# q features of batches 5 to 7 made token-major and transposed by the DMA crossbar, q of batches 0 and 1 loaded by whole rows, and a new order of all steps

## The chip, the cores and the metric

The kernel runs on one core of a Trainium2 chip. The engines of a core work side by side and meet at semaphores: PE (TensorE, matmuls; PEld is its loading of weights), DVE (VectorE), ACT (ScalarE), POOL (GpSimd) and SP (SyncE, which issues DMAs). DMAs issued from POOL and from SP run on the core's 16 DMA engines. The metric is the device time of one execution in microseconds (us), as a median of several runs. A profile is one further execution; its span is the time from its first to its last instruction.

## What is computed

The reference is a linear attention with an exponential feature map, followed by a feed-forward network with a squared ReLU.

```python
# q, k, v: 8 batches x 8 heads x 576 tokens x 64;  w_phi: 64 x 128
def phi(x):
    proj = np.einsum('bhsd,df->bhsf', x, w_phi)
    proj = proj - np.max(np.abs(proj), axis=-1, keepdims=True)
    return np.concatenate([np.exp(proj), np.exp(-proj)], axis=-1)
q_p, k_p = (phi(q), phi(k))
kv = np.einsum('bhsf,bhsd->bhfd', k_p, v)
z = np.sum(k_p, axis=2)
num = np.einsum('bhsf,bhfd->bhsd', q_p, kv)
den = np.einsum('bhsf,bhf->bhs', q_p, z)[..., None] + 1e-06
# then, with the heads side by side as x: 4608 tokens x 512
h = np.maximum(x @ w_in, 0.0)          # w_in: 512 x 2048
out = (h * h @ w_out).astype(np.float32)   # w_out: 2048 x 512
```

## The kernel before, in words

**Tiles.** A batch has 576 tokens and eight heads. Two heads lie side by side in 128 columns, so a batch of q or k is 18 blocks of 128 tokens by 128 columns: 16 for the first 512 tokens and two for the last 64 tokens of all heads. Loads are issued from POOL and turn float32 into bf16 on the way (`load`, L253 for the 512 tokens and L261 for the 64). The code speaks of five groups `c` (of q) or `g` (of k) in a batch: four of four blocks, and the last, number 4, of two blocks with the 64 tokens.

**Attention, `attention(b)`.** For each batch:
- q and k are turned so that the 64 features of a head lie on partitions. Batches 0 and 1 do this on PE (`pe_transposes`, L328, with a copy out by DVE or ACT); from batch 2 on it is one DMA transpose through the crossbar for each of q and k, issued from SP (`transposed`, L338).
- For k, `project` (L354; L381 in batch 0) multiplies by w_phi with tokens on the output's partitions ("token-major"); DVE takes the largest absolute value of each token and head (L409), ACT makes the two exponentials kp and kn (L415, L397 in batch 0). v is scaled by the exponential of the maximum (L442, on DVE; batches 0 and 1 may do it on POOL), and `kv_ops` (L472, L477) gives kv and z.
- For q, `qmax_ops` makes the same token-major projection (L354, L507 in batch 0) only for DVE's maximum (L514) and a small exponential of it, `en`; the bank is free after that. `q_ops` then makes the projection a second time, with the 128 features on partitions ("feature-major", L549, two matmuls of 512 columns for a group), and ACT makes qp and qn of it (L564, twice).
- `out_ops` multiplies qp with kv (NA, L579), DVE scales by `en` (L591), qn with kv is added (NB, L579), DVE takes the reciprocal of the denominator (L599) and divides (L603), and the result xo is transposed into xT by a DMA on SP (L637; in batch 0 on PE, L619 and L628). The last 64 tokens of all batches go to xS.

**Feed-forward.** Chunk c holds batch c's first 512 tokens; chunk 8 holds the 64 last tokens of all batches. F1 (L719; L730 for chunk 0 in pieces) multiplies by w_in; ACT or DVE takes the ReLU (L694, L696), DVE or, in chunks 0 and 1, POOL squares it (L703); F2 (L784; L748 for the last tile in halves) multiplies by w_out, and ACT or DVE copies the result out (L195, L197) for a store from SP (L803, L800, L771). The FFN of chunk c stands between the attention of later batches.

**The order.** The code above only lists steps with what they read and write (`add`). The order in which they are issued is a written-out list, `ORDER`; each engine takes its steps in that order and waits at each until its inputs are there. `BASES` gives each PSUM bank group its bank, `STATES` picks one of two engines for the steps that have a choice, `GATES` makes a load of batch 2 and later wait for a named step, and `FILL` puts idle matmuls (L853) on a tile of zeros ahead of some PE steps. The numbers in `add`'s cost field serve the search that wrote the list; they do not run.

**q's loads in batches 0 and 1 (`load_q`, L284).** They come in halves: token pairs 0 and 1 of each row of four first (128 of 256 columns), then pairs 2 and 3. From batch 2 on q is loaded in four pieces of whole rows (L273).

## Time and profile before

| | |
|---|---|
| median of 3 runs | 355.15 us (354.94 to 355.79) |
| profiled execution: span, first to last instruction | 353.0 us |
| instructions in the span | 8396 |
| PE busy | 340.7 us, 97% of the span |
| DVE busy | 276.1 us, 78% |
| ACT busy | 226.8 us, 64% |
| POOL busy | 96.6 us, 27% |
| DMA packets | 96101, 39.59 MB, mean 112 GB/s |
| granted TensorE clock | 1.000 |

For the profiled execution itself the profile gives the span of 353.0 us; it stands 2.15 us under the median of the runs.

How to read it: the page gives the busy time of each engine, then the span in 40 slices with one digit for each engine (9 means busy for 90% or more), then the DMA queues, then the chain of work that ended last, followed back from the last instruction, and then the costliest groups of instructions. In a group, `out<-in` are the program's tile names, then partitions x elements and type, the count, and after the first bar the busy time in us and the mean of one instruction in ns; after the second bar stands the idle time of the engine ahead of them, and what ended it. A timeline line has the start in us, the duration in us, engine, line, operation, tiles and count. An SP or POOL line with a DMA is its issue; the landing is later.

### The profile page before, as it was taken

Reading aid. Unit: us, or ns where it says so; the run is one execution under the profiler, and the core shown is the slowest. Engines: PE = TensorE matmul, PEld = TensorE weight load, DVE = VectorE, ACT = ScalarE, POOL = GpSimd, SP = SyncE. Lnnn points to the kernel's source line nnn. Section 1 sums busy time; section 2 is a strip of 40 time slices with the busy share of each in tenths; the row PEclk is TensorE's granted clock in tenths of the full one; section 3 lists DMA queues with packets and bytes.
Section 4 is the critical chain, followed back from the end, with each engine's and each line's share of the span. In section 5 each row is a group of like instructions: output and inputs, shape, how many; then the busy total and the mean of one; then the engine's idle time right before and its main releaser. Section 6 shows DMA issues by size and latency. Waiting matters only on the chain.

```text
span 353.0 us, 8396 instructions
## 1 busy us (share of the span) xinstructions
PE 340.7 (97%) x3367; PEld 192.2 (54%) x3400; DVE 276.1 (78%) x524; ACT 226.8 (64%) x428; POOL 96.6 (27%) x144
## 2 busy tenths in 40 slices
PE   8889999999999999999999999999999999999995
PEld 5679875544654554545445654455555544444452
DVE  4999998899979988989678888799988727736210
ACT  4999887499688875785678577869676211340301
POOL 8745350488429300297001820000000000000000
PEclk9999999999999999999999999999999999999999
DMA  9999999899989976899354995600211211010105
GB/s 102 177 200 202 196 107 155 134 142 175 182 169 150 155 141 155 160 111 158 79 129 84 120 187 111 146 20 21 53 40 53 47 51 48 30 59 2 59 3 176
DMA packets 96101, 39.59 MB, mean 112 GB/s; under 512 B 64576, under 2 KB 91584, under 8 KB 96064
## 3 DMA queue, kind: packets, MB, share of 16 engines
q0 software_dynamic: 45216, 18.36, 45.6%
q1 hardware_dynamic: 50528, 20.42, 26.5%
q8 instruction: 26, 0.43, 0.5%
q10 hardware_dynamic: 320, 0.30, 0.3%
q14 instruction: 11, 0.09, 0.1%
HBM read 36.77 MB, written 9.44 MB: 131 GB/s over the span
## 4 chain that ended last, share of the span: by engine, by line
PE 79%; DVE 8%; ACT 6%; DMA 3%; issue 2%; SPq 0%; POOL 0%; DVEq 0%; ACTq 0%; POOLq 0%
PE psum L784 30%; PE psum L719 28%; PE psum L579 5%; PE psum L354 4%; PE psum L472 3%; PE psum L730 3%; PE psum L549 2%; DVE va L442 2%; DMA xq<-in_q_dram 1%; DVE mq L514 1%; ACT kp L415 1%; ACT kn L415 1%; DMA out_dram<-ot 1%; DVE mk L388 1%; DVE h L703 1%
## 5 line engine op out<-in xcount | busy, mean ns | idle before, releaser
L784 PE MATMUL psum<-wout,h 128*128 128x512 bf16 x527 | 128.4, 379 | 3.2 <-issue 1.3
L719 PE MATMUL psum<-xT,win 128*128 128x512 bf16 x448 | 106.1, 379 | 0.1
L694 ACT ACTIVATE hr<-psum 128x512 bf16<-128x512 f32 x96 | 55.3, 596 | 46.3 <-PE psum L719 24.3
L784 PEld LDWEIGHTS <-h 128*128 128x128 bf16 x560 | 50.2, 98 | 55.2 <-issue 2.0
L719 PEld LDWEIGHTS <-win 128*128 128x128 bf16 x512 | 47.4, 97 | 53.7 <-issue 3.1
L703 DVE TENSOR_TENSOR h<-hr 128x512 bf16<-128x512 bf16 x143 | 55.9, 415 | 16.4 <-ACT hr L694 15.6
L564 ACT ACTIVATE qp<-psum 128x1024 bf16<-128x1024 f32 (+1 forms) x40 | 37.4, 940 | 21.9 <-PE psum L549 21.5
L514 DVE TENSOR_REDUCE mq<-psum 128x8 f32<-128x1024 f32 (+1 forms) x40 | 44.1, 1110 | 4.0 <-PE psum L354 3.2
L409 DVE TENSOR_REDUCE mk<-psum 128x8 f32<-128x1024 f32 (+1 forms) x35 | 38.1, 1110 | 3.1 <-PE psum L354 3.1
L415 ACT ACTIVATE kp<-psum 128x1024 bf16<-128x1024 f32 (+1 forms) x35 | 32.8, 937 | 11.6 <-DVE mk L409 8.9
L564 ACT ACTIVATE qn<-psum 128x1024 bf16<-128x1024 f32 (+1 forms) x40 | 37.4, 939 | 1.3 <-PE psum L579 1.0
L696 DVE TENSOR_SCALAR hr<-psum 128x512 bf16<-128x512 f32 x48 | 32.6, 686 | 6.5 <-PE psum L719 5.2
L253 POOL DMA_DIRECT2D xv<-in_v_dram x26 | 19.4, 763 | 51.3 <-DVE va L442 48.0
L415 ACT ACTIVATE kn<-psum 128x1024 bf16<-128x1024 f32 (+1 forms) x35 | 32.8, 936 | 0.0
L442 DVE TENSOR_TENSOR va<-xv,va 64x256 bf16<-64x256 bf16 (+2 forms) x68 | 30.4, 462 | 1.6 <-ACT va L434 0.8
L591 DVE TENSOR_TENSOR psum<-psum,en 128x520 f32<-128x520 f32 (+1 forms) x40 | 27.6, 699 | 3.9 <-PE psum L579 2.5
L603 DVE TENSOR_TENSOR xo<-psum,rden 128x512 bf16<-128x512 f32 (+1 forms) x40 | 27.3, 686 | 1.0 <-DVE rden L599 0.2
L197 ACT ACTIVATE ot<-psum 128x512 f32<-128x512 f32 x18 | 10.7, 595 | 27.1 <-PE psum L784 27.1
L195 DVE COPY ot<-psum 128x512 f32<-128x512 f32 x17 | 11.5, 684 | 15.2 <-PE psum L784 7.9
L253 POOL DMA_DIRECT2D xk<-in_k_dram x28 | 20.6, 743 | 8.4 <-ACT va L428 4.0
L472 PE MATMUL psum<-va,kp 128*128 128x65 bf16 x256 | 19.6, 193 | 0.8 <-DVE va L442 0.4
L472 PE MATMUL psum<-va,kn 128*128 128x65 bf16 x256 | 19.6, 193 | 0.0
(69 smaller groups left out, 403.4 us busy)
## 6 DMA issues: line engine op xcount, KB each, us to landing
out_dram<-ot SPq DMA_DIRECT2D x32, 256.0 KB, 2.7
xk<-in_k_dram POOLq DMA_DIRECT2D x26, 128.0 KB, 4.3
xq<-in_q_dram POOLq DMA_DIRECT2D x24, 128.0 KB, 5.5
xv<-in_v_dram POOLq DMA_DIRECT2D x24, 128.0 KB, 4.2
win<-in_moe_w_in_dram POOLq DMA_DIRECT2D x4, 512.0 KB, 11.3
wout<-in_moe_w_out_dram POOLq DMA_DIRECT2D x4, 512.0 KB, 11.7
xq<-in_q_dram POOLq DMA_DIRECT2D x4, 256.0 KB, 5.8
xv<-in_v_dram POOLq DMA_DIRECT2D x2, 512.0 KB, 9.3
```

Of the source, the lines that this page charges most:

```text
L253: pin(nc.gpsimd.dma_start(out=x[:, a * 512 : z * 512].rearrange("p (h x) -> p h x", x=4 * D), in_=src[b][2 * a : 2 * z, 0:512, :].rearrang ...
L409: pin(nc.vector.tensor_reduce(out=mk_view(g), in_=ps2(pj)[:, :, : n * Fd].rearrange("p e (i f) -> p e i f", f=Fd), axis=AX.X, op=ALU.max, ...
L415: pin(nc.scalar.activation(out=dst[slot][:, :, :n, :].rearrange("p e i f -> p e (i f)"), in_=ps2(pj)[:, :, : n * Fd], func=ACT.Exp, scale= ...
L442: pin(engine().tensor_tensor(out=t[:, :, :D].rearrange("p m (x c) -> p m x c", c=2), in0=x.rearrange("p (m x c) -> p m x c", m=n, c=2), in ...
L472: pin(nc.tensor.matmul(out=o[:, sg, hi, :], lhsT=(kp, kn)[sg][kgroup[pr]][:, j % 2, 2 * hi + j // 2, :], rhs=va[s2][sg][:, 8 * pr + 4 * hi ...
L514: pin(nc.vector.tensor_reduce(out=mqb[:, c, :, :n], in_=ps2(pj)[:, :, : n * Fd].rearrange("p e (i f) -> p e i f", f=Fd), axis=AX.X, op=ALU ...
L564: pin(nc.scalar.activation(out=o, in_=i_, func=ACT.Exp, scale=sgn))
L694: pin(nc.scalar.activation(out=hr[sl], in_=ps1(g), func=ACT.Relu))
L696: pin(nc.vector.tensor_scalar(out=hr[sl], in0=ps1(g), scalar1=0.0, scalar2=None, op0=ALU.max))
L703: pin(engine().tensor_tensor(out=dst, in0=i_, in1=i_, op=ALU.mult))
L719: pin(nc.tensor.matmul(out=o, lhsT=win[mc // 4][:, kc, mc % 4 * P : (mc % 4 + 1) * P], rhs=x, start=(kc == 0), stop=(kc == KC - 1)))
L784: pin(nc.tensor.matmul(out=ps1(g), lhsT=h2[c % 2][mc // 4][:, mc % 4, tt * P : (tt + 1) * P], rhs=wout[mc // 4][:, mc % 4, :], start=(mc = ...
```

## The change

- In batches 5 to 7 (`LATE`), a q group's second, feature-major projection is gone. Instead, `qmax_ops` keeps the bank of the token-major projection after the maximum, and ACT makes both exponentials of it into a tile `qe` (two of them, in turn). One DMA transpose from SP (step Xf) turns its 16 blocks of 128x128 into the feature-major `qf`, of which qp and qn are now the two halves; for the last group of a batch it is two transposes of four blocks. In these batches `qmax_ops` stands beside `out_ops` group by group.
- q of batches 0 and 1 is loaded like k, in whole rows; batch 0's in two pieces of two head pairs. PE's transposes of q take the blocks in the order that this gives.
- The ring of k feature tiles has 6 slots for 7. The tile of the last output half lies over the first `qe`; an unused tile is dropped.
- `ORDER`, `BASES`, `STATES`, `GATES` and `FILL` are new throughout. By the new `STATES` and order, POOL has 17 squares (1 before) and 8 scalings of v (0 before), the ReLUs are 92 on ACT and 52 on DVE (96 and 48 before), kv's copies 23 and 9 (19 and 13), the output copies 20 and 15 (18 and 17). `FILL` has 28 idle matmuls (76 before). POOL's first load is k's head pairs 2 and 3 of batch 0 (256 KB in bf16); before it was head pair 0 (128 KB).

```diff
--- before.py
+++ after.py
@@ -165,7 +165,7 @@
     warm = sb("warm", [256])
     xk, xq, xv = ring("xk", 2, [36 * D]), ring("xq", 2, [36 * D]), ring("xv", 2, [36 * D])
     kT, qT = ring("kT", 2, [18, P]), ring("qT", 2, [18, P])
-    NKP = 7
+    NKP = 6
     kp, kn = ring("kp", NKP, [2, 4, P]), ring("kn", NKP, [2, 4, P])
     va = [[sb(f"va{b}{s}", [40, D1 + 1]) for s in range(2)] for b in range(2)]
     mk, mq = ring("mk", 2, [36], F32), ring("mq", 2, [5, 2, 4], F32)
@@ -175,16 +175,17 @@
     NXT = 2
     LENT = 2
     assert B * S == NCH * TCH and NCH == B + 1 and S == TCH + 64
-    qp, qn = ring("qp", NQP, [8 * P]), ring("qn", NQP, [8 * P])
+    LATE, NQE = 5, 2
+    qf, qe = ring("qf", NQP, [2, 8 * P]), ring("qe", NQE, [2, 8 * P])
+    qp, qn = [t[:, 0, :] for t in qf], [t[:, 1, :] for t in qf]
     xo = ring("xo", 5, [8 * D])
     rden = ring("rden", 5, [8], F32)
     xT = [ring(f"xT{c}", 2, [4, 2, P]) for c in range(NXT)]
     xS = sb("xS", [4, KC, P])
-    mkn = sb("mkn", [36], F32)
     hr = ring("hr", 4, [TCH])
     h2 = [ring(f"h2{c}_", 4, [4, TCH]) for c in range(2)]
     ot = ring("ot", 3, [DM], F32)
-    otl = sb("otl", [DM], F32)
+    otl = qe[0][:, 0, :].bitcast(F32)
 
     plan = Plan()
     add = plan.add
@@ -264,36 +265,12 @@
                 add("POOL", (0.72, 0), fn, w=[(tag, b % 2, "s", hi)], dma=(LD["s"], SW_IN, "ld", late(b)),
                     release=release, what=tag + "s")
 
-    def load_q(b, jjs=(0, 1), single=True, release=False, prs=((0, 4),)):
-
-        x = xq[b % 2]
-        if b >= 2:
-            for a, z in prs:
-                def fn(a=a, z=z):
-                    pin(nc.gpsimd.dma_start(
-                        out=x[:, a * 512 : z * 512].rearrange("p (h x) -> p h x", x=4 * D),
-                        in_=q[b][2 * a : 2 * z, 0:512, :].rearrange("h (p j) d -> p h (j d)", j=4)))
-                old = sorted({pr // 2 for pr in range(a, z)}) if b < 4 else []
-                add("POOL", (0.72, 0), fn, w=[("xq", b % 2, "g", pr) for pr in range(a, z)] + [("xq", b % 2, jj) for jj in old]
-                    + [("xq", b % 2, jj, y) for jj in old for y in range(3)],
-                    dma=(work(b, LD["main"] * (z - a) / 4), SW_IN, "ld", late(b)), release=release, what="xq")
-            jjs = ()
-        for jj in jjs:
-            for a, z in prs:
-                def fn(jj=jj, a=a, z=z):
-                    pin(nc.gpsimd.dma_start(
-                        out=x[:, jj * 1024 + a * 256 : jj * 1024 + z * 256].rearrange("p (h x) -> p h x", x=128),
-                        in_=q[b][2 * a : 2 * z, 0:512, :].rearrange("h (p j) d -> p h (j d)", j=4)[:, :, jj * 128 : jj * 128 + 128]))
-                add("POOL", (0.72, 0), fn, w=([("xq", b % 2, jj)] if z == 4 else []) + [("xq", b % 2, jj, y) for y in range(a, min(z, 3))],
-                     dma=(work(b, LD["main"] / 8 * (z - a)), SW_IN, "ld", late(b)), release=release, what="xq")
-        if single:
-            load(q, xq, b, "xq", prs=(), release=release)
+    def load_q(b, single=True, release=False, prs=((0, 4),)):
+
+        load(q, xq, b, "xq", prs=prs, single=single, release=release)
 
     def of(tag, b, us):
-        if tag == "xq" and b >= 2:
-            return [(tag, b % 2, "g", pr) for pr in range(4)] + [(tag, b % 2, "s", hi) for hi in range(2)]
-        qs = [("xq", b % 2, u, a) for u in us if u != "s" for a in range(3)] if tag == "xq" else []
-        return qs + [(tag, b % 2, u) for u in us if u != "s"] + [(tag, b % 2, "s", hi) for u in us if u == "s" for hi in range(2)]
+        return [(tag, b % 2, u) for u in us if u != "s"] + [(tag, b % 2, "s", hi) for u in us if u == "s" for hi in range(2)]
 
     def load_win(i):
         def fn():
@@ -308,7 +285,7 @@
         add("POOL", (0.72, 0), fn, w=[("wout", i)], dma=(LD["w"], SW_IN, "ld", "first"), what="wout")
 
 
-    kslot, qslot, xslot = [0], [0], [0]
+    kslot, qslot, xslot = [0], [0, 0], [0]
 
     def t_of(g):
         return [16, 17] if g == 4 else [4 * g + i for i in range(4)]
@@ -325,6 +302,8 @@
             def fn():
                 tp = ps1(g).bitcast(BF16)
                 for i, t in enumerate(blocks):
+                    if tag == "xq" and t < 16:
+                        t = t % 8 * 2 + t // 8
                     pin(nc.tensor.transpose(out=tp[:, i * P : (i + 1) * P], in_=x[:, t * P : (t + 1) * P], identity=ident))
             add("PE", pe_cost(n, 0.056), fn, r=of(tag, b, srcs) + ["ident"], opens=g, w=[g], what="T" + tag)
             def fn():
@@ -336,7 +315,7 @@
         def transposed(x, xt, tag, ttag):
             def fn():
                 pin(nc.sync.dma_start_transpose(out=xt, in_=x))
-            add("SP", (2.8 if tag == "xk" else 3.4, 0), fn, r=of(tag, b, (0, 1, "s") if tag == "xq" else (0, 1, 2, 3, "s")),
+            add("SP", (2.8 if tag == "xk" else 3.4, 0), fn, r=of(tag, b, (0, 1, 2, 3, "s")),
                 w=[(ttag, s2, t) for t in range(18)], dma=(3.6, HW_IN, "x", "kq"), what="X" + tag)
 
         if not pe_in:
@@ -496,6 +475,8 @@
                 return [8 * (c // 2) + h for h in range(8)]
             return [(8 * (c // 2) + 4 * (c % 2) + i) if pe_in else 8 * (c % 2) + 2 * i + c // 2 for i in range(4)]
 
+        qfeat = {}
+
         def qmax_ops(c):
             ts = q_ts(c)
             n = min(len(ts), 4)
@@ -514,7 +495,32 @@
                 pin(nc.vector.tensor_reduce(
                     out=mqb[:, c, :, :n], in_=ps2(pj)[:, :, : n * Fd].rearrange("p e (i f) -> p e i f", f=Fd),
                     axis=AX.X, op=ALU.max, apply_absolute_value=True))
-            add("DVE", dve_cost(2 * n * Fd), fn, r=[pj], w=[("mq", s2, c)], closes=pj, what="Mq")
+            turned = b >= LATE
+            add("DVE", dve_cost(2 * n * Fd), fn, r=[pj], w=[("mq", s2, c)] + [pj] * turned, closes=None if turned else pj, what="Mq")
+            if turned:
+                slot, se = qslot[0] % NQP, qslot[1] % NQE
+                qslot[0] += 1
+                qslot[1] += 1
+                qfeat[c] = slot
+                for u, sgn in enumerate((1.0, -1.0)):
+                    def fn(u=u, sgn=sgn):
+                        i_, o = ps2(pj)[:, :, : n * Fd], qe[se][:, u, : 2 * n * Fd]
+                        if c == 4:
+                            o, i_ = o.rearrange("p (i e f) -> p e i f", e=2, f=Fd), i_.rearrange("p e (i f) -> p e i f", f=Fd)
+                        else:
+                            o = o.rearrange("p (e x) -> p e x", e=2)
+                        pin(nc.scalar.activation(out=o, in_=i_, func=ACT.Exp, scale=sgn))
+                    add("ACT", act_cost(2 * n * Fd), fn, r=[pj], w=[pj, ("qe", se, u)], closes=pj if u else None, what="Eq")
+                def fn():
+                    if c == 4:
+                        for u in range(2):
+                            pin(nc.sync.dma_start_transpose(out=qf[slot][:, u, : 4 * P].rearrange("f (x p) -> f x p", p=P),
+                                                            in_=qe[se][:, u, : 4 * Fd]))
+                    else:
+                        pin(nc.sync.dma_start_transpose(out=qf[slot].rearrange("f u (x p) -> f (u x) p", p=P),
+                                                        in_=qe[se].rearrange("p u x -> p (u x)")))
+                add("SP", (2.5 if c < 4 else 2.0, 0), fn, r=[("qe", se, u) for u in range(2)], w=[("qp", slot), ("qn", slot)],
+                    dma=(3.2 * n / 4, HW_IN, "x", "kq"), what="Xf")
 
             if c < 4:
                 def fn():
@@ -528,8 +534,6 @@
                             out=enb[0:64, 4, :].rearrange("p (i e h) -> p e i h", e=2, h=2)[:, :, :, hi],
                             in_=mqb[64 * hi : 64 * hi + 64, 4, :, :2], func=ACT.Exp, scale=-2.0))
                     add("ACT", act_cost(4), fn, r=[("mq", s2, 4)], w=[("en", s2, 4, hi)], what="en")
-
-        qfeat = {}
 
         def q_ops(c):
             ts = q_ts(c)
@@ -647,7 +651,7 @@
             for jj in range(2):
                 for hh in range(2):
                     ts = [8 * jj + 4 * hh + i for i in range(4)]
-                    pe_transposes(xq[s2], "xq", "qT", ts, [jj], qTb[:, ts[0] : ts[-1] + 1, :])
+                    pe_transposes(xq[s2], "xq", "qT", ts, [2 * hh, 2 * hh + 1], qTb[:, ts[0] : ts[-1] + 1, :])
             pe_transposes(xq[s2], "xq", "qT", [16, 17], ["s"], qTb[:, 16:18, :])
             qmax_ops(0)
             q_ops(0)
@@ -663,7 +667,7 @@
                 for jj in range(2):
                     for hh in range(2):
                         ts = [8 * jj + 4 * hh + i for i in range(4)]
-                        pe_transposes(xq[s2], "xq", "qT", ts, [jj], qTb[:, ts[0] : ts[-1] + 1, :])
+                        pe_transposes(xq[s2], "xq", "qT", ts, [2 * hh, 2 * hh + 1], qTb[:, ts[0] : ts[-1] + 1, :])
                 pe_transposes(xq[s2], "xq", "qT", [16, 17], ["s"], qTb[:, 16:18, :])
             for g in (4, 0, 1, 2, 3):
                 kgroup_ops(g)
@@ -677,10 +681,14 @@
             v_ops(2, 4)
             kv_ops(2)
             kv_ops(3)
+            if b < LATE:
+                for c in range(5):
+                    qmax_ops(c)
             for c in range(5):
-                qmax_ops(c)
-            for c in range(5):
-                q_ops(c)
+                if b < LATE:
+                    q_ops(c)
+                else:
+                    qmax_ops(c)
                 out_ops(c)
 
 
@@ -812,9 +820,8 @@
 
     add("POOL", (0.45, 0.6), f_ident, r=["ident0"], w=["ident"], what="ident")
     load(k, xk, 0, "xk", prs=((1, 2), (2, 4)), single=False)
-    load_q(0, jjs=(0,), single=False)
+    load_q(0, prs=((0, 2), (2, 4)))
     load(v, xv, 0, "xv", prs=((0, 4),))
-    load_q(0, jjs=(1,))
     for i in range(4):
         load_win(i)
     load(k, xk, 1, "xk")
@@ -858,120 +865,116 @@
 
 
 ORDER = [
-    4, 3, 0, 1, 5, 9, 13, 15, 2, 6, 12, 8, 14, 40, 10, 41, 11, 7, 42, 64, 44, 43, 19, 65, 46, 18, 66, 45, 109, 16,
...
+    4, 3, 14, 12, 1, 5, 74, 9, 0, 11, 85, 13, 6, 2, 86, 75, 76, 78, 8, 87, 39, 89, 79, 77, 88, 90, 10, 63, 40, 15,
...
 ]
 BASES = (
...
 )
 STATES = (
...
 )
 GATES = {
...
 }
 FILL = {
-    40: (0, 15, 0), 42: (0, 3, 0), 64: (0, 4, 0), 66: (0, 6, 0), 109: (0, 3, 0), 144: (0, 6, 0), 53: (0, 5, 0),
-    77: (3, 2, 0), 155: (7, 19, 0), 158: (7, 5, 0), 127: (2, 2, 0), 149: (6, 1, 0), 161: (6, 5, 0),
+    74: (3, 15, 0), 76: (3, 1, 0), 41: (3, 4, 0), 52: (2, 3, 0), 140: (5, 4, 0), 132: (4, 1, 0),
 }
```

15 lines of the change are left out of this document (7 added, 8 removed), and 188 rows, old and new, of tables (GATES, ORDER).

## The prediction

> **What bounds the kernel now.** I read the page first: busy time, slices, chain.
>
> ```profile
> span 353.0 us, 8396 instructions
> PE 340.7 (97%) x3367; PEld 192.2 (54%) x3400; DVE 276.1 (78%) x524; ACT 226.8 (64%) x428; POOL 96.6 (27%) x144
> ...
> DVE  4999998899979988989678888799988727736210
> ACT  4999887499688875785678577869676211340301
> ...
> PEclk9999999999999999999999999999999999999999
> ...
> PE 79%; DVE 8%; ACT 6%; DMA 3%; issue 2%; SPq 0%; POOL 0%; DVEq 0%; ACTq 0%; POOLq 0%
> ```
>
> PE is busy for 97% of the span and carries 79% of the chain; its clock is granted in full throughout. DVE and ACT stand at 9 in the first slices only. So I cut the span into windows (columns: PE, weight loads, DVE, ACT, POOL busy us; clock; DMA share; GB/s).
>
> ```profile
> 0.00:25.00 25.00, 21.29 (x287) 15.91 (x288) 20.19 (x45) 19.90 (x48) 17.15 (x28) 1.00 1.29 157
> 25.00:50.00 25.00, 24.41 (x427) 21.15 (x427) 24.21 (x52) 23.18 (x44) 12.01 (x17) 1.00 1.25 173
> 50.00:75.00 25.00, 24.68 (x310) 14.64 (x311) 22.50 (x41) 16.91 (x32) 9.57 (x16) 1.00 1.10 144
> 75.00:100.00 25.00, 24.71 (x255) 13.40 (x256) 22.67 (x42) 21.50 (x39) 14.49 (x21) 1.00 1.25 170
> 100.00:150.00 50.00, 49.08 (x514) 26.35 (x518) 45.72 (x78) 37.97 (x73) 17.52 (x26) 1.00 1.01 155
> 150.00:200.00 50.00, 49.00 (x478) 25.94 (x478) 40.73 (x79) 35.50 (x67) 21.11 (x32) 1.00 0.80 114
> 200.00:250.00 50.00, 49.20 (x466) 25.62 (x470) 43.73 (x78) 37.88 (x70) 4.78 (x8) 1.00 0.53 97
> ```
>
> Three stages. Up to 50 us DVE and ACT are both nearly full: they feed PE, and PE's busy time contains fillers and short waits. From 50 to 100 us DVE is 90% full, ACT less. From 100 us on PE idles 2.7 us in 150 (0.92, 1.00 and 0.80).
>
> Prices come from the groups of the page (the last number before the second bar is the mean in ns; the last two are in the full list of groups) and from the chain, where back-to-back matmuls show their real spacing.
>
> ```profile
> L694 ACT ACTIVATE hr<-psum 128x512 bf16<-128x512 f32 x96 | 55.3, 596 | 46.3 <-PE psum L719 24.3
> L703 DVE TENSOR_TENSOR h<-hr 128x512 bf16<-128x512 bf16 x143 | 55.9, 415 | 16.4 <-ACT hr L694 15.6
> L564 ACT ACTIVATE qp<-psum 128x1024 bf16<-128x1024 f32 (+1 forms) x40 | 37.4, 940 | 21.9 <-PE psum L549 21.5
> L514 DVE TENSOR_REDUCE mq<-psum 128x8 f32<-128x1024 f32 (+1 forms) x40 | 44.1, 1110 | 4.0 <-PE psum L354 3.2
> L853 PE MATMUL psum<-warm 128*128 128x248 bf16 x76 | 11.7, 298 | 1.1 <-DVE warm L234 1.1
> L703 POOL TENSOR_TENSOR h<-hr 128x512 bf16<-128x512 bf16 x1 | 1.0, 1041 | 1.5 <-DVE hr L696 1.5
> ```
>
> ```profile
> 71.06 2.59 PE psum L719 x12
> ...
> 269.38 0.54 PE psum L549 x4
> ```
>
> A 512-column matmul costs PE 0.216 us (2.59/12). The feature product (L549, two matmuls for a token group) costs 0.27 (0.54 for two groups).
>
> **The change, part by part.** The sum is made against the profiled execution: its span is 353.0 us, and the median of the runs, 355.15, is 2.15 above it; I add that back at the end.
>
> *Feature products removed.* In batches 5 to 7, 15 groups lose their L549 products: 12 whole ones x 0.27 and 3 half ones x 0.14 = 3.7 us. They stand where PE idles 1 us in 50, so they come off the end: -3.7.
>
> *Exponentials.* Thirty activations on the token-major projection replace thirty on the feature-major one, same size (0.94 each): ACT 0. They hold the projection's bank pair longer, through the maximum (1.11) and both exponentials, while the second pair that the feature product took is gone. Cost 0; the cover is that fewer pairs are open in all.
>
> *Fifteen crossbar steps, 18 instructions, on SP's queue.* The nearest rows are q's own transposes (18 blocks of 128x128; the new ones have 16) and the output's (4 blocks; the last group's two have 4 each):
>
> ```profile
> L338 SPq DMA_TRANSPOSE qT<-xq x6: 2671/2784/7034, 50.2 to 217.4; - x6
> ...
> DMA to landing us min/median/max: 4.6/5.3/9.7
> ```
>
> ```profile
> L637 SPq DMA_TRANSPOSE xT<-xo x28: 1188/1217/2485, 60.5 to 283.9; - x28
> ...
> DMA to landing us min/median/max: 2.3/2.7/6.5
> ```
>
> So a whole group takes some 2.5 us of SP (2.67 x 16/18) and lands 4.3 (quiet: 4.6 less a ninth of 2.67) to 9.7 us after its issue; a last group 2 x 1.2 of SP and lands after 3.5. SP gets 12 x 2.5 + 6 x 1.2 = 37 us of work more; queued behind are stores and the xo transposes, whose consumers come later. What counts is how much PE work the new order puts between a step and the numerator product that reads it. Adding PE's prices along that order: batch 5 has 10 to 15 us, batch 6 has 6.6, 9.5, 5.4, 6.6 and, in its last group, 2.0; batch 7 has 14.2, 3.4, 4.4, 6.1 and 5.9. Two fall short: batch 6's last group by 3.5 - 2.0 and batch 7's second by 4.3 - 3.4, together 2.4, of which the matmul group that is under way at the issue (0.86, half of it on average) covers part. At the median landing of 5.3 three do (4.3 us in all). Bounds 0 to 4.3; I take +1.5, since DMA is at 0.5 and less by then.
>
> *The ramp, which the new order changes most.* I add the mean durations along each engine's order up to two places that the trace times by DVE's reciprocals, batch 0's last token group and batch 2's first:
>
> ```profile
> 41.35 0.19 DVE L599 RECIPROCAL rden<-psum 64x8 f32<-64x8 f32 x1
> ...
> 92.66 0.20 DVE L599 RECIPROCAL rden<-psum 128x8 f32<-128x8 f32 x1
> ```
>
> To the first place before has 37.9 us of ACT work, 37.9 of DVE and 22.6 of PE (fillers left out): 41.35 is ACT's work plus 3.4 of start, and PE has lost 18.7. After has 42.4 of ACT, 38.5 of DVE and 25.0 of PE: ACT's work plus 3.4 gives 45.8. The first load is now k's 256 KB for two head pairs where it was 128 KB for one:
>
> ```profile
> 1.25 1.55 POOL L253 DMA_DIRECT2D xk<-in_k_dram  x2 [0.80 <-POOLq L989]
> 4.44 0.24 PEld L328 LDWEIGHTS <-xk 128*128 128x128 bf16 x4 [0.57 <-DMA xk<-in_k_dram]
> ```
>
> The first 128 KB took 3.2 us to use; the second half of a 256 KB load is bounded by its share of the issue, 1.55/2 = 0.8, above and 0 below; I take 0.8. So 46.6, and PE has lost 21.6: +2.9. Between the two places before has 50.5 of DVE work in 51.3 us against 48.6 of PE: DVE sets the pace, and PE loses 2.7. After has 36.9 of DVE (16 squares and 8 scalings of v go to POOL) and 37.4 of ACT against 40.8 of PE: PE sets the pace, nothing is lost. I take -2.0 of the 2.7, since some short waits will stay. Ramp: +0.9; bounds -2 (ACT's start hidden) to +4 (DVE's relief worth nothing, some more waits).
>
> *POOL.* Sixteen squares x 1.04 and eight scalings (six as long as a square, two of twice its length): 25 us, nearly all before 100 us. POOL is busy for 53 us of that time, so it stays under 80; queued behind each are loads, of which those of win and wout stand ten and more groups ahead of their first matmul. Cost 0 where these arrive on time; bounds below under the rivals.
>
> *Fillers.* 48 of 76 go, 48 x 0.105 (248 columns at 0.216/512) = 5.0 us of PE. All lie before 28 us, where PE waits for ACT and DVE: 0 on the path. If PE was bound there they would give up to -5.
>
> *q of batches 0 and 1 by whole rows*: the same bytes in runs twice as long. The half-row loads landed in 5.8 us, a 256 KB load of k in 5.7:
>
> ```profile
> xq<-in_q_dram POOLq DMA_DIRECT2D x4, 256.0 KB, 5.8
> ...
> xk<-in_k_dram POOLq DMA_DIRECT2D x1, 256.0 KB, 5.7
> ```
>
> So 0, covered by ACT's backlog. Six k slots for seven (a batch fills five) and the last output tile laid over the first feature buffer, read by then: 0.
>
> *After 100 us.* some 11 us of DVE work are gone: its sum stands 15 us above PE's in the order of before at 100 us and 5 to 8 above it in the new one, so part of the 2.7 us of idle PE goes: -1.2 (bounds -2.7 and 0).
>
> Sum: -3.7 + 1.5 + 0.9 - 1.2 = -2.5; span 350.5, time 352.65, say 352.6.
>
> **A rule beside the rows.** In the trace one square ran on POOL (1.04 us, listed above), and nothing shows a DVE instruction held up by it. The Trainium skill, SBUF — State Buffer, section "Who interferes with whom", says that a DVE instruction with two SBUF inputs contends with a GpSimd instruction that reads SBUF, and that the later one waits for the whole of the earlier. Squares and scalings of v are of that kind on both engines. No row shows such a pair; what it would make of the time is the third rival.
>
> In all windows the granted clock is 1.00, with 76 fillers in the order. The Trainium skill, TensorE: Matmul & The Clock Gate, Part 1, says that a monitor halves the clock when PE was idle over a window of 3.4 us; by it fewer fillers may cost clock in the ramp. That is the last rival.
>
> **Rivals.**
> - *More than the forecast.* The idle 2.7 us after 100 us and the whole DVE-bound loss of 2.7 go (ramp +2.9 - 2.7), and the transposes cost 0.5: -3.7 - 2.7 + 0.2 + 0.5 = -5.7, some 349.4. For it: DVE's digits of 9 thin out. Against: a new order has its own short waits.
> - *The freed PE time is not used.* ACT, which has 42.4 us before batch 0 is out, idles on its way (it is idle 5.1 of the first 25 us now) and the ramp costs +3.4 instead of +0.9; 355.1, no change.
> - *The transposes come late* (the other side). Place: each of the 15 numerator products. SP serves in order, and a step that waits for its exponentials holds up the next ones and the outputs' transposes, which gate the next chunk. Without the 1.5 the sum is -4.0, so it decides from an average PE wait of 0.27 us a group; at 0.5 the time is 355.15 - 4.0 + 7.5 = 358.6. For it: landings up to 9.7 and an SP issue of 7.0 in a loaded stretch. Against: DMA's share falls from 0.80 to 0.53 in those windows.
> - *DVE and POOL collide.* 24 POOL instructions, each holding up a DVE one by half its length: 12.5 us of DVE. At batch 2's first group DVE has 75.4 + 4 of start against PE's 65.8 + 21: 7 us of room. Beyond 7 it decides; 12.5 gives 352.6 + 5.5 = 358.1. Against: most of DVE's time there is on PSUM.
> - *The clock falls in the ramp.* Assume, beyond what any row shows, that a third of the 25 us of PE work up to batch 0's end took twice as long: +8, of which PE's slack under ACT hides half; 356.6. Against: PE would still work for more than half of that stretch.
>
> **How the numbers follow.** Forecast 0.45 (own range 350.8 to 354.4); more 0.17; unused 0.14; late transposes 0.10; collision 0.09; clock 0.05. The time is the forecast's, 352.6. Leaving out a tenth at each end, the range goes from 348.5, a little under the second case, to 358.3, at the costly ones. A difference of 0.3% is 1.07 us, about what a measurement can tell from no change: faster is below 354.1. The forecast gives faster 0.41 and same 0.04, the second case 0.17, the unused case 0.02, 0.10 and 0.02, the rest slower: faster 0.60, same 0.14, slower 0.26.
>
> **What would show it.** Right: no L549-like products after batch 4; PE's busy time about 5 + 3.7 less; first FFN matmuls (L730 before) from about 29 us on; batch 0's last reciprocal near 46 us and batch 2's first some 42 us later; DVE under 85% from 50 to 100 us; PE's waits for feature buffers 1 to 3 us in all. Wrong: waits of PE on the new transposes above 4 us, DVE squares longer than 0.42 beside POOL's, a granted clock under 1.00, or ACT idle more than 6 us before batch 0's last group.

## Result and profile after

The changed kernel takes 373.47 us (median of 4 runs, 371.40 to 377.89) where the kernel before takes 355.25: 1.048 times as long, with a 95% interval of 1.045 to 1.052. Some executions fall into a slower state: medians here are over all executions, ratios and their intervals leave the slow ones out, and differences between kernels are taken from the ratios. The prediction said 352.6, and its range ended at 358.3. The profiled execution took 373.79 us, with a span of 372.0.

The page of the changed kernel, the lines that answer to those shown of before (the clock's digits are tenths of the full clock):

```profile
span 372.0 us, 8388 instructions
PE 347.8 (94%) x3322; PEld 195.6 (53%) x3322; DVE 278.1 (75%) x499; ACT 227.0 (61%) x429; POOL 123.0 (33%) x167
...
DVE  3999994789988698829798899888877764555330
ACT  3989937488676678638658985866875703112101
...
PEclk9869969999999899989999999999999999999999
...
PE 75%; DVE 10%; DMA 5%; issue 4%; ACT 4%; SPq 0%; DVEq 0%; POOLq 0%
```

PE does not work for as large a share as before, its clock falls in a few slices of the first half, and DVE is not relieved: it is busy for 278.1 us where it was 276.1, although some 11 us of its instructions went to POOL. The same windows as in the prediction (PE, weight loads, DVE, ACT, POOL busy us; clock; DMA share; GB/s):

```profile
0.00:25.00 25.00, 20.09 (x172) 13.80 (x173) 18.34 (x37) 17.77 (x40) 20.31 (x30) 0.81 1.22 153
25.00:50.00 25.00, 20.79 (x395) 18.05 (x393) 23.81 (x37) 20.94 (x42) 20.68 (x25) 0.98 1.08 144
50.00:75.00 25.00, 23.44 (x324) 17.38 (x324) 17.08 (x35) 14.82 (x31) 13.35 (x19) 0.87 1.43 150
75.00:100.00 25.00, 21.57 (x188) 10.53 (x187) 23.87 (x32) 19.38 (x34) 18.68 (x25) 1.00 1.29 180
100.00:150.00 50.00, 47.98 (x502) 25.57 (x502) 42.10 (x74) 36.83 (x70) 24.30 (x34) 0.97 0.97 119
150.00:200.00 50.00, 46.06 (x431) 23.71 (x426) 38.36 (x70) 32.29 (x59) 15.96 (x24) 0.97 0.93 135
200.00:250.00 50.00, 50.00 (x483) 26.58 (x482) 44.26 (x78) 37.52 (x72) 7.68 (x11) 1.00 0.86 155
```

All is lost in the first 200 us, most of it in the first 100. From 200 us on, in batches 5 to 7 with the crossbar part, PE has no idle time at all (50.00 of 50, where before had 49.20). The two places that the prediction timed, batch 0's last reciprocal and batch 2's first (41.35 and 92.66 before):

```profile
53.87 0.20 DVE L603 RECIPROCAL rden<-psum 64x8 f32<-64x8 f32 x1
...
103.81 0.27 DVE L603 RECIPROCAL rden<-psum 128x8 f32<-128x8 f32 x2
```

So 12.5 us are lost up to the first, and 11.2 up to the second. The timeline of DVE, POOL and PE around 46 us shows the largest single piece (start, duration, and in brackets the idle time before and what ended it):

```profile
44.71 0.67 DVE L704 TENSOR_SCALAR hr<-psum 128x512 bf16<-128x512 f32 x1
45.31 4.82 DVE L711 TENSOR_TENSOR h<-hr 128x512 bf16<-128x512 bf16 x1
50.05 1.21 DVE L495 TENSOR_REDUCE mq<-psum 128x8 f32<-128x1024 f32 x1
```

```profile
45.99 3.84 POOL L421 TENSOR_TENSOR va<-xv,va 128x1024 bf16<-128x1024 bf16 x2
```

```profile
46.55 0.41 PE L583 MATMUL psum<-kv,qf 128*128 128x65 bf16 x8
51.31 1.87 PE L738 MATMUL psum<-xT,win 128*128 128x128 bf16 x16 [4.35 <-DVE mq L495]
```

One square on DVE, 0.41 us elsewhere, stands for 4.82 us until two scalings of v on POOL are through. Behind it in DVE's queue is a maximum over q (L495), and PE waits 4.35 us for that. When PE resumes, 16 matmuls of 128 columns take 1.87 us where they took 1.06 earlier in the same run (at 32.58 us): its clock is halved (granted clock 0.50 from 50 to 55 us). That is a reading of one place; the runs below test whether it is the cause.

### The profile page after: what moved, and what is told of

The parts are those of the page before. It is cut to its first block, busy times and chain, and to the rows that moved or that the text cites. A ratio compares the mean times of both kernels' runs of the same rounds, so it can differ in the third digit from the quotient of the medians.

```text
span 372.0 us, 8388 instructions
## 1 busy us (share of the span) xinstructions
PE 347.8 (94%) x3322; PEld 195.6 (53%) x3322; DVE 278.1 (75%) x499; ACT 227.0 (61%) x429; POOL 123.0 (33%) x167
## 4 chain that ended last, share of the span: by engine, by line
PE 75%; DVE 10%; DMA 5%; issue 4%; ACT 4%; SPq 0%; DVEq 0%; POOLq 0%
PE psum L792 28%; PE psum L727 27%; PE psum L583 5%; DMA xT<-xo 4%; PE psum L333 4%; PE psum L451 4%; PE psum L738 3%; DVE mq L495 2%; DVE va L421 2%; ACT qf L568 1%; DMA xk<-in_k_dram 1%; DVE mk L388 1%; PE psum L553 1%; PE psum L307 1%; DVE mk L367 1%
## 5 line engine op out<-in xcount | busy, mean ns | idle before, releaser
L792 PE MATMUL psum<-wout,h 128*128 128x512 bf16 x560 | 134.7, 380 | 0.2 <-DVE h L711 0.2
L727 PE MATMUL psum<-xT,win 128*128 128x512 bf16 x448 | 110.3, 386 | 6.7 <-DMA xT<-xo 5.8
L702 ACT ACTIVATE hr<-psum 128x512 bf16<-128x512 f32 x92 | 53.9, 595 | 75.2 <-PE psum L727 50.8
L711 DVE TENSOR_TENSOR h<-hr 128x512 bf16<-128x512 bf16 x127 | 57.6, 473 | 11.5 <-ACT hr L702 10.7
L568 ACT ACTIVATE qf<-psum 128x1024 bf16<-128x1024 f32 (+1 forms) x50 | 45.0, 936 | 12.7 <-PE psum L553 12.0
L704 DVE TENSOR_SCALAR hr<-psum 128x512 bf16<-128x512 f32 x52 | 35.4, 685 | 14.9 <-PE psum L727 12.9
L495 DVE TENSOR_REDUCE mq<-psum 128x8 f32<-128x1024 f32 (+1 forms) x40 | 44.2, 1110 | 3.1 <-PE psum L333 3.0
L583 PEld LDWEIGHTS <-qf 128*128 128x128 bf16 x640 | 29.0, 98 | 14.1 <-issue 2.3
L595 DVE TENSOR_TENSOR psum<-psum,en 128x520 f32<-128x520 f32 (+1 forms) x40 | 27.7, 703 | 9.2 <-PE psum L583 6.8
L254 POOL DMA_DIRECT2D xq<-in_q_dram x27 | 19.8, 734 | 41.7 <-ACT kp L394 7.8
L583 PE MATMUL psum<-kv,qf 128*128 128x65 bf16 x640 | 32.3, 195 | 0.8 <-DVE mq L495 0.3
L512 ACT ACTIVATE qe<-psum 128x1024 bf16<-128x1024 f32 (+1 forms) x30 | 27.5, 939 | 6.3 <-DVE mq L495 6.1
L198 ACT ACTIVATE ot<-psum 128x512 f32<-128x512 f32 x20 | 11.6, 593 | 19.2 <-PE psum L792 15.5
## 6 DMA issues: line engine op xcount, KB each, us to landing
wout<-in_moe_w_out_dram POOLq DMA_DIRECT2D x4, 512.0 KB, 11.2
```

The source lines that it names most:

```text
L254: pin(nc.gpsimd.dma_start(out=x[:, a * 512 : z * 512].rearrange("p (h x) -> p h x", x=4 * D), in_=src[b][2 * a : 2 * z, 0:512, :].rearrang ...
L495: pin(nc.vector.tensor_reduce(out=mqb[:, c, :, :n], in_=ps2(pj)[:, :, : n * Fd].rearrange("p e (i f) -> p e i f", f=Fd), axis=AX.X, op=ALU ...
L568: pin(nc.scalar.activation(out=o, in_=i_, func=ACT.Exp, scale=sgn))
L583: pin(nc.tensor.matmul(out=o[:, u // 4, u % 4 * D1 : (u % 4 + 1) * D1], lhsT=(qp, qn)[sg][slot][:, u * m : u * m + P], rhs=kv_sb[s2][:, h ...
L702: pin(nc.scalar.activation(out=hr[sl], in_=ps1(g), func=ACT.Relu))
L704: pin(nc.vector.tensor_scalar(out=hr[sl], in0=ps1(g), scalar1=0.0, scalar2=None, op0=ALU.max))
```

## Experiments

The theory: 25 steps on POOL (17 squares, 8 scalings of v) and DVE's own squares and scalings hold each other up. Rivals: the clock that falls; the new order itself with its loads; the crossbar part. The plan decides by one digit for each movable step whether its second engine does it; the experiments that name engines change these digits alone.

**GpSimd's steps put back on VectorE.** First all 25, then the scalings alone (one hunk of the digits):

```diff
-    '0000101111101000010110001010001100001100010101011001000000010001011100100100110010110000000110010001'
+    '0000100000000000010110001010001100000000000000001000000000000000001000100100100010100000000100000000'
```

> The changed kernel with its 25 GpSimd steps (17 squares, 8 scalings of v) put back on VectorE, in the same order. Theory of the collision (VectorE instructions with two inputs wait for GpSimd's, one of them 4.82 us where 0.41 is usual, and TensorE stands for 4.35 us behind it): the 4.82 us instruction goes, the square's mean falls from 473 to about 415 ns, TensorE's long gap near 47 us goes; VectorE gets 17 x 0.42 + 8 x 0.7 = 12.7 us more work, a part of which shows; 360 to 366. Rival, the order itself (too little work for TensorE and late loads in the first 60 us, whoever does the squares): 371 to 378, with a gap of several us still there before 60 us.

> The changed kernel with its 8 scalings of v back on VectorE, the 17 squares left on GpSimd. If the two scalings of 1.96 us in front of the one stretched square are the main harm of the collision: that square is back at 0.41, TensorE's gap of 4.35 us near 47 us and the half clock behind it (about 2 us) go: 366 to 369. If all the small collisions count, as much is still lost and it stays at 370 to 373. If the order is the cause: 372 to 376.

Measured: all 25 back, 365.84 us (1.026 times before, 1.020 to 1.032); the scalings alone, 370.07 (1.038, 1.031 to 1.045). In all_on_vector the square that took 4.82 us takes 0.40, and PE's longest wait of the first 100 us is 1.3 us, for its first load:

```profile
44.64 0.40 DVE L711 TENSOR_TENSOR h<-hr 128x512 bf16<-128x512 bf16 x1
```

In its groups squares and scalings have the means of the kernel before again (changed kernel first, then this one; the number before the last bar is the mean in ns):

```profile
L711 DVE TENSOR_TENSOR h<-hr 128x512 bf16<-128x512 bf16 x127 | 57.6, 473 | 11.5 <-ACT hr L702 10.7
...
L421 DVE TENSOR_TENSOR va<-xv,va 64x256 bf16<-64x256 bf16 (+2 forms) x60 | 30.7, 528 | 2.2 <-ACT va L407 0.8 <-ACT va L413 0.6
L595 DVE TENSOR_TENSOR psum<-psum,en 128x520 f32<-128x520 f32 (+1 forms) x40 | 27.7, 703 | 9.2 <-PE psum L583 6.8 <-ACT qe L512 1.0 <-ACT en L527 0.6
```

```profile
L711 DVE TENSOR_TENSOR h<-hr 128x512 bf16<-128x512 bf16 x144 | 56.6, 413 | 11.7 <-ACT hr L702 10.9
...
L421 DVE TENSOR_TENSOR va<-xv,va 64x256 bf16<-64x256 bf16 (+2 forms) x68 | 30.0, 462 | 2.0 <-ACT va L407 0.8 <-ACT va L413 0.4
L595 DVE TENSOR_TENSOR psum<-psum,en 128x520 f32<-128x520 f32 (+1 forms) x40 | 27.6, 701 | 9.7 <-PE psum L583 7.2 <-ACT qe L512 1.0 <-ACT en L527 0.6
```

Beside POOL the 127 squares cost 127 x 60 ns = 7.6 us more and the 60 scalings 60 x 66 ns = 4.0 us: 11.6 us, about as much as went to POOL. (The scalings' mean mixes three sizes; with the sizes kept apart the sum is the same 4.0 us.) The stretch is uneven: three squares of 4.82, 2.12 and 1.26 us hold 7.0 of the 7.6. L595, which has one input in PSUM, keeps its time. Some 8 of the 17 us come back with the 25 steps, so the rest is elsewhere. The scalings alone bring some 4, but their executions range from 366.5 to 373.8 us, so this share is rough.

**The same 25 steps on GpSimd in the kernel before.** Nothing else is touched, digits again; then the 17 squares alone.

> The kernel before, nothing moved in its order, but the same 25 steps on GpSimd as in the changed kernel (17 squares of the first two groups of tokens, 8 scalings of v of batches 0 and 1). Theory of the collision: VectorE's squares and scalings lengthen, GpSimd issues loads later, and some 12 of the changed kernel's 18 us come back: 363 to 370. Rival (GpSimd's help is good or neutral, the harm is in the order): 352 to 357.

> The kernel before with the 17 squares on GpSimd and the 8 scalings of v left on VectorE. With all 25 it took 20 us longer. If harm goes with GpSimd's busy time (18 of 28 us): 365 to 369. If the scalings of v in the ramp do most of it (they stand before the first products with v, two behind each other, 1.3 us each): 357 to 363.

Measured: 374.78 us with all 25 (1.056, 1.054 to 1.058), 365.37 with the squares (1.029, 1.026 to 1.031). So the squares cost 10 us and the scalings another 9, though they are fewer; the expectation was too low for all 25. A stretch of its ramp, DVE and then POOL; in the kernel before eleven of these scalings take 3.75 us there:

```profile
17.86 6.98 DVE L442 TENSOR_TENSOR va<-xv,va 64x256 bf16<-64x256 bf16 x6
```

```profile
17.18 2.17 POOL L442 TENSOR_TENSOR va<-xv,va 128x512 bf16<-128x512 bf16 x2
...
20.11 2.08 POOL L442 TENSOR_TENSOR va<-xv,va 128x512 bf16<-128x512 bf16 x2
...
22.94 1.07 POOL L442 TENSOR_TENSOR va<-xv,va 128x512 bf16<-128x512 bf16 x1
```

Six scalings on DVE take 6.98 us among five on POOL. In an order that was good without them, POOL's steps cost more than the whole change does. Not all of this is stretched work of DVE. PE's longest waits in this run (us in total, times, longest):

```profile
PE psum L477 <- DVE va L442: 5.0, 2, 2.6
PE psum L784 <- POOL h L703: 4.3, 2, 2.4
PE psum L472 <- POOL va L442: 3.0, 2, 1.9
```

For 7.3 us PE waits for POOL's own squares and scalings. A square takes POOL 1.10 us where it takes DVE 0.42, and POOL's loads stand between them. In the changed kernel no wait of PE ends with a step of POOL; there the harm goes through DVE.

**The dispute measured by itself.** Sixty GpSimd instructions that nobody reads, behind the last load of the kernel before: once multiplications, once memsets.

```diff
+    dm = sb("dm", [512])
...
+        if 1290 <= at < 1650 and at % 6 == 0:
+            now[0] = idle
+            pin(nc.gpsimd.tensor_tensor(out=dm, in0=dm, in1=dm, op=ALU.mult))
```

> The kernel before with 60 multiplications on GpSimd that nobody needs (a 128x512 tile by itself, nothing waits for them) behind its last load, so some 63 us of unbroken GpSimd work from about 205 us on, in a stretch where VectorE is two thirds busy. Theory of the collision: VectorE instructions with two inputs from SBUF (squares, scalings of v) that fall into the stretch take 0.4 to 1.5 us longer each, copies and reductions from PSUM keep their time, and the end moves by 3 to 15 us: 358 to 370. Rival (the changed kernel's lengthened squares have another cause): all means as before, 354 to 356.

> As idle_gpsimd_multiplies, with 60 memsets of a 128x1024 tile in place of the multiplications. If it is GpSimd's two-input work that VectorE waits for: no VectorE mean changes, 354 to 356. If any GpSimd work on SBUF does it: squares lengthen here too and the time moves as with the multiplications, in proportion to GpSimd's busy time.

Measured: 369.48 us with the multiplications (1.041, 1.039 to 1.042), 354.79 with the memsets (1.001, 0.998 to 1.003). DVE's groups from 205 to 270 us, first with the multiplications, then with the memsets:

```profile
L704 DVE TENSOR_TENSOR h<-hr 128x512 bf16<-128x512 bf16 x20 | 18.2, 938 | 1.1 <-ACT hr L695 0.8
L515 DVE TENSOR_REDUCE mq<-psum 128x8 f32<-128x1024 f32 (+1 forms) x10 | 11.0, 1107 | 1.0 <-PE psum L355 1.0
L443 DVE TENSOR_TENSOR va<-xv,va 64x256 bf16<-64x256 bf16 (+1 forms) x12 | 10.7, 897 | 0.9 <-ACT va L435 0.8
...
L592 DVE TENSOR_TENSOR psum<-psum,en 128x520 f32<-128x520 f32 (+1 forms) x7 | 4.8, 700 | 0.6 <-PE psum L580 0.6
```

```profile
L515 DVE TENSOR_REDUCE mq<-psum 128x8 f32<-128x1024 f32 (+1 forms) x10 | 11.0, 1112 | 1.4 <-PE psum L355 1.4
L704 DVE TENSOR_TENSOR h<-hr 128x512 bf16<-128x512 bf16 x27 | 10.4, 416 | 1.8 <-ACT hr L695 1.7
...
L443 DVE TENSOR_TENSOR va<-xv,va 128x1024 bf16<-128x1024 bf16 (+1 forms) x16 | 7.6, 482 | 0.9 <-ACT va L435 0.8
L592 DVE TENSOR_TENSOR psum<-psum,en 128x520 f32<-128x520 f32 (+1 forms) x9 | 6.2, 700 | 0.4 <-PE psum L580 0.2
```

Beside 66 us of multiplications a square takes 938 ns instead of 416, a scaling about twice its time (1217 instead of 688 ns for the large ones, 668 instead of 276 for the small); reductions and everything with an input in PSUM keep theirs; 57 us of memsets (951 ns each) change nothing. So the collision is shown: DVE's instructions with two inputs in SBUF are held up by GpSimd's multiplications, and not by its memsets. Whether it is the reading of SBUF that makes the difference between the two, or something else in which a multiplication differs from a memset, these runs do not separate. The Trainium skill, SBUF — State Buffer, section "Who interferes with whom", states just this pair, and that an instruction which only writes does not take part; the trace agrees on both (938 against 416 ns, and no change beside memsets).

**The clock.** 33 more fillers before seven PE steps of the first 26 us, once in the changed kernel and once in all_on_vector (the entries of the list, drawn together into lines):

```diff
-    74: (3, 15, 0), 76: (3, 1, 0), 41: (3, 4, 0), 52: (2, 3, 0), 140: (5, 4, 0), 132: (4, 1, 0),
+    74: (3, 24, 0), 76: (3, 1, 0), 41: (3, 4, 0), 52: (2, 3, 0), 140: (5, 4, 0), 132: (4, 1, 0),
+    108: (3, 5, 0), 110: (1, 5, 0), 114: (3, 3, 0), 118: (1, 3, 0), 218: (7, 5, 0), 224: (1, 3, 0),
```

> The changed kernel with 33 more filler multiplications before seven TensorE steps of the first 26 us. Theory of the clock (half clock from 15 to 26 us because TensorE stood idle in the 15 us before it): the granted clock of 15 to 30 us goes from 0.66 to above 0.9, batch 0's first reciprocal comes 3 to 5 us earlier than 30.2 us, 367 to 371. Rival (the first 30 us are set by VectorE and ScalarE, and the clock is only a companion): the clock may rise, the reciprocal stays within 1 us of 30.2, 372 to 375.

> all_on_vector with the 33 fillers of more_fillers. Without a collision in the ramp the clock should now stay at 0.9 or above in 15 to 30 us. If the half clock holds 3 to 5 us of the ramp: 360.5 to 363.5, batch 0's first reciprocal ahead of 28.8 us. If VectorE and ScalarE set the ramp: the clock rises and the reciprocal stays, 364 to 367.

Measured: 372.79 us and 366.77, so nothing gained in either. In the first a collision of five scalings (19.19 to 24.63 us) stopped PE, and the clock fell there. The second is clear; the window of 15 to 30 us and batch 0's first reciprocal, without the fillers and with them:

```profile
15.00:30.00 15.00, 13.89 (x181) 10.13 (x179) 14.81 (x31) 13.55 (x33) 5.21 (x9) 0.68 1.24 176
```

```profile
28.77 0.20 DVE L603 RECIPROCAL rden<-psum 128x8 f32<-128x8 f32 x1
```

```profile
15.00:30.00 15.00, 11.38 (x189) 8.47 (x186) 14.62 (x29) 12.63 (x31) 5.30 (x9) 1.00 1.24 176
```

```profile
29.19 0.20 DVE L603 RECIPROCAL rden<-psum 128x8 f32<-128x8 f32 x1
```

The clock goes from 0.68 to 1.00, and the reciprocal comes 0.4 us later. In the next pair of runs, again without and with the fillers, the same reciprocal stands at 28.53 and 30.57 us, so it is no earlier there either. DVE is busy for 14.6 to 14.8 of the 15 us in both rows above: by that it sets the pace of these 15 us, and the half clock is a companion there.

**Loads among transposes.** What else holds all_on_vector back: from 100 to 180 us PE waits only for transposes of attention rows (xT), and these were in flight together with loads for batch 6. Six of these loads get a later place in POOL's order and a later gate (only the gates are shown):

```diff
-    1160: 797, 1164: 793, 1165: 798, 1166: 675, 1167: 627, 1168: 627,
+    1160: 901, 1164: 901, 1165: 901, 1166: 901, 1167: 901, 1168: 901,
```

> all_on_vector with six loads of batch 6 (four of 256 or 128 KB pieces of q and k, two short ones) issued behind the third group's fourth activation, some 10 us later, out of the way of the four transposes of attention rows. If these transposes are late because of the loads: TensorE's wait of 3.8 us near 147 us goes below 1.5, the transposes land within 4 us, 360 to 364. If it is the queue's order: the wait stays, 364 to 368.

> Both edits. If both hold their part: 356 to 360, near the kernel before; if neither does: 364 to 368.

Measured: 364.06 us, and 360.68 with the fillers too (1.015, 1.013 to 1.018). PE's waits on these transposes from 100 to 180 us, in all_on_vector and in vector_and_later_loads (sum, times, longest):

```profile
PE psum L727 <- DMA xT<-xo: 4.1, 2, 3.8
```

```profile
PE psum L727 <- DMA xT<-xo: 0.4, 1, 0.4
```

The wait goes as expected, and the median landing of these transposes falls from 5.2 to 4.0 us. The time does not follow beyond the noise: 1.025 (1.022 to 1.027) after 1.026 (1.020 to 1.032). In the profiled run of vector_and_later_loads PE waited elsewhere, 3.6 us at 74 us for q's transposes of another batch. With the fillers too that wait is 1.8 us, and the time falls by some 4 us against all_on_vector, to just above the range expected for both. Why fillers help only beside later loads isn't settled. The ramp's reciprocal, no earlier with them, doesn't show it. One difference stands further on: from 60 to 100 us the granted clock is 0.91 with the later loads alone and 1.00 with both, and behind its wait at 74 us PE works on without a break. So a half clock may well cost time there, some 3 us by an estimate (40 x 0.09 = 3.6 us of clock, of which PE idled for a part). No run takes this apart.

**The crossbar part.** In the changed kernel this part alone is undone (the feature product and its two exponentials stand again, between the places of the token-major exponentials and of the crossbar step):

```diff
-    LATE, NQE = 5, 2
+    LATE, NQE = 8, 2
...
-    otl = qe[0][:, 0, :].bitcast(F32)
+    otl = sb("otl", [DM], F32)
```

> The changed kernel, its order, loads and GpSimd steps untouched, with the crossbar part alone undone: for the 15 query groups of batches 5 to 7 the feature product on TensorE (512 columns twice, then two exponentials) stands again where the token-major exponentials and the crossbar step were. If the crossbar part is good or neutral, as the loss that stands still from 180 us on says: 374 to 378 (12 x 0.27 + 3 x 0.14 = 3.7 us of TensorE work come back). If it does harm: 366 to 372.

Measured: 388.57 us (383.53 to 390.99; 1.085, 1.079 to 1.092), by the ratios some 13 more than the changed kernel and above both expectations. The windows up to 180 us and behind, changed kernel first:

```profile
0.00:180.00 180.00, 159.99 (x1802) 98.40 (x1802) 145.16 (x246) 128.93 (x249) 105.70 (x142) 0.93 1.11 141
180.00:350.00 170.00, 169.94 (x1428) 88.08 (x1428) 128.46 (x245) 95.89 (x176) 17.31 (x26) 1.00 0.61 115
```

```profile
0.00:180.00 180.00, 158.79 (x1815) 97.65 (x1816) 146.92 (x248) 128.92 (x250) 105.67 (x142) 0.92 1.15 141
180.00:350.00 170.00, 163.16 (x1385) 82.71 (x1382) 122.17 (x231) 92.69 (x170) 17.28 (x25) 1.00 0.38 70
```

The first stretch is alike; behind it PE idles 6.8 us where it idled 0.06. So nothing says that the crossbar part slows the kernel: with it PE is full from 180 us on. How much it is worth can't be read from the 13 us: the old steps stand in an order that was not made for them, and PE now waits on their exponentials and maxima.

> The kernel before, in its own order, loads and engines, with the crossbar part alone: q features of batches 5 to 7 token-major, 15 crossbar steps, 15 x 2 exponentials, six k slots. The loss against TensorE's own work stood still in the changed kernel from 180 us on, so the part should keep most of the 3.7 us of TensorE work that it takes away: 351.0 to 354.0, with the first 150 us as before. Rival (the crossbar steps hold the queue, or features land late, in an order that was not made for them): above 355.5, with TensorE waiting on feature tiles from 160 us on.

The other way round, the part alone in the kernel before, gave 387.31 us, a miss: PSUM banks were dealt out anew for it, and from 190 us on PE waits on activations, copies and scalings that stand ahead of its steps in this order. Some 4 of the 32 us are lost before that, by 93 us already, where the part itself has not begun. (With the banks dealt out anew this kernel's results come out changed, which is put down to fillers that write into banks with sums of batch 0; the amount of work is the same.) It tells nothing of the part itself.

**Splices.** Before's order up to a step, the changed order behind it:

> The first 300 steps of the kernel before (some 47 us: its ramp, its loads of q by column halves, its 76 fillers, all of it on VectorE), and behind them the steps left in the changed kernel's order, with its crossbar part and its 13 remaining GpSimd steps. If the harm is done in the ramp (half clock, late loads, the stretched square at 45 us): 356 to 361. If the rest of the first 180 us costs as much by itself: 364 to 370.

> The first 540 steps of the kernel before (some 100 us), then the changed order with the crossbar part, all squares and scalings on VectorE. If order and GpSimd of the first 100 us are all the harm: 350 to 355, since the crossbar part takes 3.7 us from TensorE. If the changed order's own stall behind 140 us (transposes queued behind a crossbar step of q that waits for its loads, 7 us) stays: 356 to 360.

> As first_100_of_before, but with the first 760 steps of the kernel before (some 140 us), so past the loads that the changed order's crossbar steps wait for. Theory (the crossbar part is good, the harm lies ahead of it): 348.5 to 353. Rival (the crossbar part costs what it saves, or the late order is worse): 355 and more.

Measured: 383.67, 376.28 and 367.24 us, all above every expectation. The seams lie at about 48, 89 and 128 us, so the last two names promise more than they hold. Up to the seam each is as fast as before (the third falls 2.0 us behind from 108 us on), and behind it PE stands on freed banks, activations and transposes of q (5.6 us for one of them in the second). An order is made as a whole; its halves don't fit another's, and these runs decide nothing between ramp and rest.

## Why the prediction was wrong

The step that failed is *POOL*: "cost 0 where these arrive on time". It named the loads behind POOL's steps as what could suffer. The loads were not it: PE waits for one of them alone, the first, for 1.5 us. DVE's own squares and scalings were, by 11.6 us in all, and some 8 us come back when the 25 steps leave POOL. (The part's own sum is also short: 16 x 1.04 + 6 x 1.04 + 2 x 2.08 is 27 us, not 25; the 25 steps took 28.0.) This takes with it, in part:

- *The ramp* (+0.9 predicted). Batch 0's last reciprocal came at 53.87, not 46.6, and batch 2's first 49.9 us later, not some 42. By the busy time not ACT's work was the pace, but DVE's: from 25 to 50 us it is busy for 23.81 us, of which the one square holds 4.4 in vain. POOL's steps are not the whole of it. In all_on_vector batch 2's first reciprocal stands at 95.39 us, so 8.4 of the 11.2 us lost up to there are gone, but batch 0's last is only 4.1 us earlier, still 3.2 later than predicted:

```profile
49.79 0.19 DVE L603 RECIPROCAL rden<-psum 64x8 f32<-64x8 f32 x1
```

- *DVE's relief* (-2.0 up to 100 us, -1.2 behind). None came: 276.1 us before, 278.1 after.

*The rival "DVE and POOL collide"* was the mechanism, and its 12.5 us of stretched DVE time (13.5 with the sum put right) were near the 11.6 measured. That is partly luck: it spread half a length over each of 24 instructions, where three squares hold 7.0 us. It fell short in two ways. Its chance was set at 0.09 because most of DVE's time has an input in PSUM; that is so, but the steps that do not came together in the ramp. And of its 12.5 us it let 7 disappear in DVE's room, a sum over 100 us. In fact single instructions stretch by up to 4.4 us, and PE waits for what is queued right behind them, however much room the window has elsewhere: some 8 us came back when the steps went back, and in the kernel before they cost 20, there with 7.3 us of PE's waits on POOL itself. The one row that the prediction had, a single square on POOL that held up nobody, said nothing of pairs.

- *Feature products removed* (-3.7): the 15 products are gone, and PE is full from 200 us on. Nothing speaks against the size, but no run shows it alone.
- *Crossbar steps* (+1.5, bounds 0 to 4.3): 0. PE never waits on them; a whole group took SP 1.62 us (median) where 2.5 was derived from q's transposes, and landed after 3.8 where 4.3 to 9.7 was allowed:

```profile
L520 SPq DMA_TRANSPOSE qf<-qe x12: 1467/1624/2763, 192.8 to 293.6; - x12
...
DMA to landing us min/median/max: 3.6/3.8/7.6
```

- *Transposes late* was a rival for these steps. The mechanism came true for other ones: the attention rows' transposes among loads, 5.8 us of PE's waits in the changed kernel. The prediction counted the loads' bytes and not what else is in flight beside them.
- *Fillers* (0): right as far as the ramp goes. Bringing 33 back gains nothing by itself; beside later loads they go with some 3 us, not explained. *The clock* did fall, as that rival said (0.81 in the first 25 us), but in the ramp, where DVE sets the pace, no cost of it shows. It can cost where PE works without a break: in the changed kernel it does so at half clock from 51.3 to 56.5 us, behind the gap of 4.35 us, which is up to 2.6 us (an estimate, half of that stretch). The Trainium skill, TensorE: Matmul & The Clock Gate, Part 1, ties the half clock to an idle window of some 3.4 us. The trace agrees only roughly: in that gap the clock halves at 49.7 us, 2.7 us after PE's last matmul. It doesn't at 15.6 us, where the clock halves in the changed kernel with no gap of PE above 0.6 us in the 9 us before. From 12.5 us on PE's only work there is transposes (L307, 1.5 us in all); whether these count for the clock no run shows.
- *The first load* (+0.8): PE starts on it at 5.89 us instead of 4.44, so 1.4. *q by whole rows, six k slots, the shared output tile* (0): no wait on them shows, but no run took them apart.

So of some 17 us (ratio 1.048), 8 lie on POOL's steps (down to 1.026), 4 on later loads and fillers together (down to 1.015), and 5.5 stay open. They arise in the first 100 us: PE idles 12.1 of these in vector_loads_and_fillers and 4.9 in the kernel before, but only 1.2 of the 250 us that follow. Batch 0's first reciprocal is late already, 25.08 us before and 30.57 here; that this is the same 5.5 us is chance, since in all_on_vector, with the same ramp but for the fillers, it is late by 3.7.

```profile
25.08 0.19 DVE L599 RECIPROCAL rden<-psum 128x8 f32<-128x8 f32 x1
```

```profile
30.57 0.20 DVE L603 RECIPROCAL rden<-psum 128x8 f32<-128x8 f32 x1
```

What in the new ramp costs these 5.5 us (the first load of 256 KB, q by whole rows, the order of its steps) was not tried apart.

## What to carry to other kernels

Before an elementwise step moves from VectorE to GpSimd, look at its inputs: with two operands in SBUF it stops VectorE's instructions of the same kind, and it takes longer itself. Twenty-five such steps of 1.1 to 1.9 us cost this kernel 20 us by both together, in an order that was good without them. Price a stall by what is queued behind it at that moment, not by an engine's idle share of a long window. And an idle copy of the suspected work, which nobody waits for, tells a collision from all else in one pair of runs.

## What was not expected of the hardware

A DVE instruction caught between GpSimd instructions does not always get in after the first: one square waited through two scalings (4.82 us, against two of 1.92), though by the profile, whose times on POOL are rough, it had started 0.7 us ahead of them. Beside single-tile multiplications in an unbroken row squares took 0.94 us on average and 1.27 at most. GpSimd gives way little: its multiplications took 1.10 us beside DVE's work, against 1.04 for the one square before. Transposes by the crossbar are delayed by loads in flight: those of attention rows had a median landing of 2.7 us in the kernel before and 5.5 in the changed one, and moving six loads out of their way took it from 5.2 (all_on_vector) to 4.0.
